# Attention output stored in runs, and the second expert's output sums done chunk by chunk: a three-stage kernel on one core

## The chip, the core and the metric

The kernel runs on one core of a Trainium2 chip. The time is the device time of one execution in microseconds; several runs are made and their median is given. A profile of one execution shows what each engine did: PE (TensorE, matmuls, with the weight loads apart as PEld), DVE (VectorE), ACT (ScalarE), POOL (GpSimd) and SP (SyncE, which issues the DMAs here). PSUM is the memory that TensorE writes its results to, in banks of 512 fp32 words in each of 128 partitions; SBUF is the working memory.

## The reference

Linear attention, then a dense layer, then a layer of eight experts of which each token uses one:

```python
# attention: batch 2, 8 heads, 576 tokens, head size 64, 128 features
q_p, k_p = phi(q * scale), phi(k * scale)
num = q_p @ (k_p.T @ v);  den = q_p @ sum(k_p) + 1e-6
x = (num / den) as [1152 tokens, 512]
# dense layer, d_ff 2048
h = x @ w_in;  x = (h * sigmoid(1.702 * h)) @ w_out
# experts: 8, d_ff 1024, capacity 288
logits = x @ w_gate;  e = argmax(logits);  gate = softmax(logits)[e]
y = relu(x @ w1[e]) @ w2[e]
out = gate * y, 0 for tokens beyond the capacity
```

## The kernel before

The 1152 tokens stand in columns: `x_hi` and `x_lo` hold x with the 512 features on partitions (four chunks c) and the tokens along the free axis. Each fp32 value is kept in two parts, hi and lo, and a product takes three matmuls (`mm3`, lines 98 to 100: hi by hi, hi by lo, lo by hi).

*Attention.* Each partition loads four consecutive tokens (JF = 4) of a head, so the results come with tokens 4n + j in block j. `do_X` (line 401) transposes four blocks into a PSUM bank and hands it to `x_out` (line 397): ACT casts the bank to `x_hi` (L398), DVE takes the difference as `x_lo` (L399). The last 64 tokens of each batch go through `do_Xm`. The PSUM banks for these steps, and for the transposes and products of the attention (`t`, `nps`, `xps`), come from `mbank`, two banks in turn; a bank is free again when x_lo has been made.

*Dense layer.* Tokens are worked on in four groups of 288 (GS). For a group G and a block m of 128 hidden features, `do_h` makes twelve matmuls into `h_ps` (two banks, tag A), ACT applies the activation, and `do_y` adds the products with `w_out` to four banks, one for each output chunk of 128 features. Groups 0, 1 and 3 run interleaved, group 2 after them. For groups 1 and 3 only the logits are made; `do_logits` copies the logits out of PSUM (`lgy`, L726, for groups 0 and 2) and transposes them (L733), and `pick_slot` chooses for groups 0 and 2 the expert that is worked on.

*Experts.* For the first expert (key 0, group 0) and the second (key 1, group 2) `do_h2` makes block m of the hidden layer (twelve matmuls, then ACT's relu at L863 and DVE's lo part at L864, which releases the `h_ps` bank), and `do_y2` adds block m to all four output chunks. Eight blocks (NF2 = 8) make an expert. In the main loop `do_y2` follows `do_h2` by two blocks. The second expert's weights come in eight pieces by DMA (`eraw`), each is split by ACT (`eh`, L850) and DVE (`el`, L851). At an expert's end `do_z_out` copies the four output banks to `z`, `z_rows` transposes 96 tokens of all four chunks into a bank, and `slot_rows` (line 922) puts the rows of the chosen tokens into `base`, scales them by the gate and issues the DMA to `out`. The tile scheduler decides the order on each engine from the order in which the code is written and from the data each instruction needs.

After that the code branches past the parts for further experts, which these inputs do not need.

Of the kernel before, what the change touches and what calls it, by code (L numbers as in the profile page):

```python
# [8 lines left out]
F32 = mybir.dt.float32  # L9
# [26 lines left out]
def linear_attention__moe__top1_moe_kernel(  # L36
# [156 lines left out]

    x_hi = xp.tile([128, KD, NT], F32R, name="x_hi")
    x_lo = xp.tile([128, KD, NT], F32R, name="x_lo")
    W = {}
    def w_pair(pool, kind, i):
        t = [pool.tile([128, 4, 512], F32R, tag=f"w{kind}{i}{s}", name=f"w{kind}{i}{s}") for s in "hl"]  # L200
# [196 lines left out]
    def x_out(hi, lo, ps):  # L397
        nc.scalar.copy(hi, ps)  # L398
        nc.vector.tensor_tensor(lo, ps, hi.bitcast(F32), ALU.subtract)  # L399

    def do_X(b, p, u):

        xr = xrs.pop((b, p, u))
        ps = mbank("xps")
        for j in range(JF):
            nc.tensor.transpose(ps[:, j * 128:(j + 1) * 128], xr[:, j], ident)
        hi, lo = (t[:, 2 * p + u, b * S:b * S + SF].rearrange("p (n j) -> p j n", j=JF)
                  for t in (x_hi, x_lo))
        x_out(hi, lo, ps.rearrange("p (j n) -> p j n", j=JF))

    def do_Xm(b, p):
        ps = mbank("xps")
        for u in range(2):
            nc.tensor.matmul(ps[:, u * 64:(u + 1) * 64], xms[p][:, u], fold, start=True, stop=True)
        hi, lo = (t[:, 2 * p:2 * p + 2, b * S + SF:(b + 1) * S] for t in (x_hi, x_lo))
        x_out(hi, lo, ps[:, :128].rearrange("p (u n) -> p u n", u=2))

    npre = len(P["dec"])
    wseq = [(kd, m) for m in range(NF) for kd in ("in", "out")]
# [178 lines left out]
    def slot(n, f):  # L598
        side.setdefault(round(n * 2) / 2, []).append(f)
# [9 lines left out]
        return [gp.tile([128, GS], F32R, tag=tag, name=tag, bufs=2) for tag in ("ghi", "glo")]  # L609

    def do_h(G, m, full=False):
        tk = slice(G * GS, G * GS + GS)
        hi, lo = w_in(m)
        ps = bank("A", "h_ps")
        for c in range(KD):
            mm3(ps[:, :GS], hi[:, c], lo[:, c], x_hi[:, c, tk], x_lo[:, c, tk],
                c == 0, c == KD - 1)
        if G % 2 and not full:
            g1 = gp.tile([128, GS], F32, tag="g1", name="g1", bufs=5)
            mark["a"] = nc.scalar.activation(g1, ps[:, :GS], ACTF.Gelu_apprx_sigmoid)  # L620
# [12 lines left out]
    def do_y(G, m):  # L633
        if m == 0:
            yps[G] = y_banks()
        ghi, glo = gs.pop((G, m))
        hi, lo = w_out(m)
        for c in range(KD):
            dc = slice(c * 128, c * 128 + 128)
            mm3(yps[G][c][:, :GS], hi[:, dc], lo[:, dc], ghi, glo, m == 0, m == NF - 1)  # L640
        if m == NF - 1:
            for c in range(KD):
                sl = (slice(None), c, slice(G * GS, G * GS + GS))
                y = yps[G][c][:, :GS]
                nc.scalar.copy(x_hi[sl], y)
                nc.vector.tensor_tensor(x_lo[sl], y, x_hi[sl].bitcast(F32), ALU.subtract)

    def do_lg(G, m):


        i = G - 1 + m % 2
        if i in lgq:
            run_lg()
        lgq[i] = (m, gs.pop((G, m)))
        if len(lgq) == 4 or (G, m) == (3, NF - 1):
            run_lg()
# [59 lines left out]
    def do_logits(G):  # L716
        if G % 2 == 0:
            ps = mbank("lg_ps")
            for c in range(KD):
                tk = slice(G * GS, G * GS + GS)  # L720
                nc.tensor.matmul(ps[:2 * E, :GS], wg[:, c].rearrange("p a e -> p (a e)"), x_hi[:, c, tk],
                                 start=(c == 0), stop=False)
                nc.tensor.matmul(ps[:E, :GS], wg[:, c, 0], x_lo[:, c, tk],
                                 start=False, stop=(c == KD - 1))
            t = gp.tile([2 * E, GS], F32, tag="g1", name="lgy", bufs=5)
            nc.scalar.copy(t, ps[:2 * E, :GS])  # L726
            n = 2 * E
# [124 lines left out]

    hs, zps = {}, {}

    def do_h2(key, m, wt, tok):
        ps = bank("A", "h_ps")
        hi, lo = wt[m // 4]
        fc = slice((m % 4) * 128, (m % 4) * 128 + 128)
        for c in range(KD):
            mm3(ps[:, :GS], hi[:, c, fc], lo[:, c, fc], x_hi[:, c, tok], x_lo[:, c, tok],  # L860
                c == 0, c == KD - 1)
        hhi, hlo = parts_tile(True)
        nc.scalar.activation(hhi, ps[:, :GS], ACTF.Relu)  # L863
        nc.vector.scalar_tensor_tensor(hlo, ps[:, :GS], 0.0, hhi.bitcast(F32), ALU.max, ALU.subtract)  # L864
        hs[key, m] = (hhi, hlo)
# [10 lines left out]
    def do_z_out(key, z):  # L876
        for c in range(KD):
            if c % 2:
                nc.scalar.copy(z[:, c], zps[key][c][:, :GS])
            else:  # L880
                nc.vector.tensor_copy(z[:, c], zps[key][c][:, :GS])

    def z_rows(z, j):
        ps = mbank("zt_ps")
        for c in range(KD):
            nc.tensor.transpose(ps[:TT, c * 128:(c + 1) * 128], z[:, c, j * TT:(j + 1) * TT], ident)
        return ps[:TT, :DM]
# [102 lines left out]
    slot(NSL + NF2 + 3, lambda: slot_rows(0, 0))  # L990
    slot(NSL + NF2 + 3, lambda: slot_rows(0, 1))
    slot(NSL + NF2 + 4, lambda: slot_rows(0, 2))

    def tokens(G):
        return slice(G * GS, (G + 1) * GS)

    for n in range(NSL + 2 * NF2 + 2):
        now[0] = n
        if n < NSL:
            do_h(*seq[n])  # L1000
        elif n < NSL + 2 * NF2:
            i, m = divmod(n - NSL, NF2)
            do_h2(i, m, st[f"w{i}"], tokens(2 * i))
        for f in side.pop(n - 0.5, []):
            f()
        if 2 <= n < NSL + 2:
            do_consume(*seq[n - 2])
# [6 lines left out]
    slot_z(1)
    slot_base(1)
    for j in range(TJ):
        slot_rows(1, j)
# [5 lines left out]
    with tc.If(n_left > 0):  # L1023
# [23 lines left out]
        with tc.For_i(0, n_left):  # L1047
# [64 lines left out]
```

## Time and profile before

| | us |
|---|---|
| median of 3 runs | 340.39 (340.26 to 340.43) |
| profiled execution, its own time | 339.27 |
| its span, first to last instruction | 337.5 |
| PE busy | 318.7 (94%) |
| DVE busy | 182.9 (54%) |
| ACT busy | 172.4 (51%) |
| POOL busy | 60.4 (18%) |

The span leaves out 1.8 us of the profiled execution's time. PE's busy time counts matmuls that overlap one another, and their ends are modelled, so what it did not do is read from its idle stretches. In a row of the waits, the instruction on the left waited for the one on the right of the arrow.

### The profile page before, as it was taken

What the parts mean: (1) busy time and instruction counts of PE and PEld (TensorE: products, weight loads), DVE (VectorE), ACT (ScalarE), POOL (GpSimd) and SP (SyncE); (2) the same over time, 40 slices, a digit from 0 to 9 for tenths busy, and PEclk for the clock granted to TensorE, in tenths of its full rate; (3) what the DMA queues carried; (4) which work ended last, traced back from release to release, by engine and by line L of the source; (5) the groups of instructions that cost most, each with busy time, mean ns of one, the idle gap of its engine ahead of it and who ended that gap; (6) DMA issues with size and microseconds to landing.
All of it is one profiled execution on the core that took longest, in us unless ns stands there. A gap on an engine that the chain in (4) does not pass through costs nothing.

```text
span 337.5 us, 6635 instructions
## 1 busy us (share of the span) xinstructions
PE 318.7 (94%) x2569; PEld 304.3 (90%) x2569; DVE 182.9 (54%) x438; ACT 172.4 (51%) x445; POOL 60.4 (18%) x83
## 2 busy tenths in 40 slices
PE   5999999989997999999999999999999999999991
PEld 4999998889896999999999999989999999998990
DVE  5678797887578775444446403117434123568322
ACT  2788888879834454444444434233634233165312
POOL 3110311122003444443443410000000001010000
PEclk9999999999999999999999999999999999999998
DMA  6999541401030545435441000523400000383202
GB/s 173 296 328 271 166 134 62 127 15 50 0 105 25 186 130 172 151 122 170 124 135 64 0 2 0 156 95 94 135 23 0 2 1 2 110 271 119 72 0 80
DMA packets 29079, 35.19 MB, mean 104 GB/s; under 512 B 5360, under 2 KB 23792, under 8 KB 29040
## 3 DMA queue, kind: packets, MB, share of 16 engines
q1 hardware_dynamic: 29040, 34.69, 33.0%
q8 instruction: 22, 0.36, 0.5%
q14 instruction: 17, 0.14, 0.1%
HBM read 32.33 MB, written 2.36 MB: 103 GB/s over the span
## 4 chain that ended last, share of the span: by engine, by line
PE 82%; ACT 6%; DVE 5%; DMA 4%; issue 1%; POOL 0%; SPq 0%; ACTq 0%; DVEq 0%
PE h_ps L98 12%; PE h_ps L99 12%; PE h_ps L100 12%; PE y L98 7%; PE y L100 7%; PE y L99 7%; PE kvp L339 4%; PE nps L364 3%; DMA eraw<-in_moe_w_dram 3%; PE tp L282 2%; PE pj L98 2%; ACT x_hi L398 2%; PE t L353 2%; PE pj L99 2%; PE pj L100 2%; PE wt_ps L492 2%
## 5 line engine op out<-in xcount | busy, mean ns | idle before, releaser
L627 DVE TENSOR_TENSOR glo<-g,ghi 128x288 fp32r<-128x288 f32 x27 | 12.9, 478 | 38.7 <-ACT g L626 38.7
L236 DVE TENSOR_SCALAR wf<-wraw 128x512 int32<-128x512 int32 x32 | 16.2, 512 | 26.9 <-POOL win2l L249 10.8
L620 ACT ACTIVATE g<-h_ps 128x288 f32<-128x288 f32 x32 | 13.2, 412 | 29.4 <-PE h_ps L100 24.5
L308 DVE TENSOR_REDUCE nb<-pj 128x4 f32<-128x512 f32 (+1 forms) x40 | 25.1, 631 | 3.9 <-PE pj L100 3.5
L851 DVE TENSOR_TENSOR el<-eraw,eh 128x1024 fp32r<-128x1024 f32 x16 | 19.5, 1222 | 12.0 <-ACT eh L850 12.0
L98 PE MATMUL pj<-om_hi,xh 128*128 128x256 f32 x72 | 24.6, 341 | 1.0 <-ACT qp L321 1.0
L242 DVE SCALAR_TENSOR_TENSOR wf<-wraw,wf 128x512 int32<-128x512 int32 x32 | 25.0, 784 | 0.5
L624 ACT ACTIVATE ghi<-h_ps 128x288 fp32r<-128x288 f32 x27 | 11.1, 412 | 24.5 <-PE h_ps L100 23.9
L850 ACT CAST eh<-eraw 128x1024 fp32r<-128x1024 f32 x16 | 16.7, 1049 | 13.4 <-PE h_ps L99 7.3
L321 ACT ACTIVATE qp<-pj,nb 128x128 f32<-128x128 f32 x72 | 21.8, 389 | 0.7 <-DVE nb L308 0.5
L239 DVE SCALAR_TENSOR_TENSOR wf<-wraw,wf 128x512 int32<-128x512 int32 x32 | 21.9, 691 | 0.2
L99 PE MATMUL pj<-om_lo,xh 128*128 128x256 f32 x72 | 21.7, 301 | 0.0
L321 ACT ACTIVATE kp<-pj,nb 128x128 f32<-128x128 f32 x72 | 21.6, 394 | 0.0
L100 PE MATMUL pj<-om_hi,xl 128*128 128x256 f32 x72 | 21.4, 298 | 0.0
L285 ACT CAST xh<-tp 128x256 fp32r<-128x256 f32 (+1 forms) x40 | 14.7, 369 | 11.7 <-PE tp L282 11.7
L98 PE MATMUL h_ps<-x_hi,win0h 128*128 128x288 f32 x64 | 20.1, 314 | 0.0
L100 PE MATMUL h_ps<-x_hi,win0l 128*128 128x288 f32 x64 | 19.2, 300 | 0.5 <-POOL win0l L249 0.5
L339 PE MATMUL kvp<-vt,kp 128*128 128x65 f32 (+1 forms) x144 | 19.7, 269 | 0.0
L98 PE MATMUL h_ps<-x_hi,win3h 128*128 128x288 f32 x64 | 19.6, 306 | 0.0
L98 PE MATMUL h_ps<-x_hi,win2h 128*128 128x288 f32 x64 | 19.6, 306 | 0.0
L98 PE MATMUL h_ps<-x_hi,win1h 128*128 128x288 f32 x64 | 19.4, 303 | 0.0
L98 PE MATMUL h_ps<-x_hi,eh 128*128 128x288 f32 x64 | 19.2, 300 | 0.0
(246 smaller groups left out, 1080.5 us busy)
## 6 DMA issues: line engine op xcount, KB each, us to landing
wraw<-in_moe_w_in_dram SPq DMA_DIRECT2D x16, 512.0 KB, 4.3
wraw<-in_moe_w_out_dram SPq DMA_DIRECT2D x16, 512.0 KB, 3.6
eraw<-in_moe_w_dram SPq DMA_DIRECT2D x16, 512.0 KB, 4.7
qk_raw<-in_v_dram SPq DMA_DIRECT2D x4, 512.0 KB, 5.2
qk_raw<-in_q_dram SPq DMA_DIRECT2D x4, 512.0 KB, 5.2
qk_raw<-in_k_dram SPq DMA_DIRECT2D x3, 512.0 KB, 5.1
out_dram<-zer SPq DMA_DIRECT2D x2, 576.0 KB, 6.3
out_dram<-base SPq DMA_DIRECT2D x6, 192.0 KB, 3.0
```

The source lines that it names most:

```text
L98: nc.tensor.matmul(o, lh, rh, start=start, stop=False)
L99: nc.tensor.matmul(o, lh, rl, start=False, stop=False)
L100: nc.tensor.matmul(o, ll, rh, start=False, stop=stop)
L236: nc.vector.tensor_scalar(f, high, 3, 0x3FFFFFF8, ALU.logical_shift_left, ALU.bitwise_and)
L239: nc.vector.scalar_tensor_tensor(f, high, -0x40000000, f, ALU.bitwise_and, ALU.bitwise_or)
L242: nc.vector.scalar_tensor_tensor(f, low, 29, f, ALU.logical_shift_right, ALU.bitwise_or)
L285: nc.scalar.copy(xh[:, :n], tp[:, :n])
L308: mark["M", s] = nc.vector.tensor_reduce(nb[:, :nj], pj[:, :nj * M].rearrange("p (a m) -> p a m", m=M), AX, ALU.min)
L321: nc.scalar.activation(t[:, i], pj[:, i * M:(i + 1) * M], ACTF.Exp, bias=nb[:, i:i + 1], scale=-1.0)
L339: nc.tensor.matmul(ps[:, o:o + n], kp[:, i], vts[p][:, u, c0:c0 + n], start=(f == 0), stop=(f == NU - 1))
L850: nc.scalar.copy(hi, tv)
L851: nc.vector.tensor_tensor(lo, tv, hi.bitcast(F32), ALU.subtract)
```

## The change

Two things are changed. First, x is kept with its tokens in runs: `x_hi` and `x_lo` get the shape [128, 4, JF, 288], and token 4i + j stands at (j, i). `do_X` writes runs of 128 words; a group of 288 tokens is then four runs of 72 words, which the matmuls on x read, and y of the dense layer is written back in the same way. All results of these matmuls have the order (j, i) in PSUM; where they leave PSUM (`z`, `lgy`, the copied logits) the copy reads them in the order (i, j) and writes rows in token order.

Second, the second expert's output sums are made in a new function `do_last`: chunk c is the outer loop and block m the inner one, so all eight hidden blocks are made before, and kept in two tiles of the weight buffer `win2` (`spare`). When a chunk is done, ACT copies it to `z`; in the middle of the next chunk's sums it is transposed, put into `base`, scaled and sent out. The first expert's rows are made inside the sums of chunk 0. The last chunk is copied in three parts by DVE and leaves in two DMAs.

```diff
-    x_hi = xp.tile([128, KD, NT], F32R, name="x_hi")
-    x_lo = xp.tile([128, KD, NT], F32R, name="x_lo")
+    x_hi = xp.tile([128, KD, JF, NI], F32R, name="x_hi")
+    x_lo = xp.tile([128, KD, JF, NI], F32R, name="x_lo")
...
-        hi, lo = (t[:, 2 * p + u, b * S:b * S + SF].rearrange("p (n j) -> p j n", j=JF)
-                  for t in (x_hi, x_lo))
+        hi, lo = (t[:, 2 * p + u, :, b * BI:b * BI + 128] for t in (x_hi, x_lo))
         x_out(hi, lo, ps.rearrange("p (j n) -> p j n", j=JF))
...
-        hi, lo = (t[:, 2 * p:2 * p + 2, b * S + SF:(b + 1) * S] for t in (x_hi, x_lo))
-        x_out(hi, lo, ps[:, :128].rearrange("p (u n) -> p u n", u=2))
+        hi, lo = (t[:, 2 * p:2 * p + 2, :, b * BI + 128:(b + 1) * BI].rearrange("p u j i -> p u i j")
+                  for t in (x_hi, x_lo))
+        x_out(hi, lo, ps[:, :128].rearrange("p (u i j) -> p u i j", u=2, j=JF))
...
-            mm3(ps[:, :GS], hi[:, c], lo[:, c], x_hi[:, c, tk], x_lo[:, c, tk],
+            mm3(ps[:, :GS], hi[:, c], lo[:, c], x_hi[:, c, :, tk], x_lo[:, c, :, tk],
...
-            nc.scalar.copy(t, ps[:2 * E, :GS])
+            nc.scalar.copy(rows_of(t), in_order(ps[:2 * E, :GS]))
...
+        if key == 1 and m:
+            for s in "hl":
+                if s not in spare:
+                    spare[s] = pool_of["in", 2].tile([128, NF2 - 1, GS], F32R, tag=f"win2{s}", name=f"hh{s}")
+            hhi, hlo = spare["h"][:, m - 1], spare["l"][:, m - 1]
+        else:
+            hhi, hlo = parts_tile(True)
...
+    def do_last(wt):
+        z, base = scratch(1)
+        nc.gpsimd.memset(base, 0.0)
+        zps[1] = y_banks()
...
+        def chunk(c):
+            dc = slice(c * 128, c * 128 + 128)
+            ps = mbank("zt_ps")
+            for j in range(TJ):
+                nc.tensor.transpose(ps[:TT, j * 128:(j + 1) * 128], z[:, c, j * TT:(j + 1) * TT], ident)
+            nc.vector.copy_predicated(base[:, :, dc], mk.unsqueeze(2).to_broadcast([TT, TJ, 128]),
+                                      ps[:TT, :TJ * 128].rearrange("p (j d) -> p j d", j=TJ))
+            nc.vector.tensor_tensor(base[:, :, dc], base[:, :, dc],
+                                    gw[:, g0:g0 + TJ].unsqueeze(2).to_broadcast([TT, TJ, 128]), ALU.mult)
+            nc.sync.dma_start(out=rows[:, :, dc], in_=base[:, :, dc])
+        half = NF2 // 2
+        for c in range(KD):
+            sums(c, range(half))
+            if c:
+                chunk(c - 1)
+            else:
+                slot_rows(0, 0)
+                slot_rows(0, 1)
+            sums(c, range(half, NF2))
+            if c == 0:
+                slot_rows(0, 2)
+            if c < KD - 1:
+                nc.scalar.copy(rows_of(z[:, c]), in_order(zps[1][c][:, :GS]))
...
+        for j in range(TJ):
+            nc.vector.tensor_copy(rows_of(zl[j]), in_order(zps[1][c][:, :GS])[:, j * TT // JF:(j + 1) * TT // JF])
+        for j, ps in enumerate(pss):
+            nc.tensor.transpose(ps[:TT, 0:128], zl[j], ident)
+            nc.vector.copy_predicated(base[:, j, dc], mk[:, j:j + 1].to_broadcast([TT, 128]), ps[:TT, 0:128])
+            if j < TJ - 1:
+                nc.scalar.activation(base[:, j, dc], base[:, j, dc], ACTF.Copy, scale=gw[:, g0 + j:g0 + j + 1])
+            else:
+                nc.vector.tensor_scalar(base[:, j, dc], base[:, j, dc], gw[:, g0 + j:g0 + j + 1], None, ALU.mult)
+        nc.sync.dma_start(out=rows[:, 0, dc], in_=base[:, 0, dc])
+        nc.sync.dma_start(out=rows[:, 1:, dc], in_=base[:, 1:, dc])
```

In the attention the order on every engine stays as it is. In the second expert it changes. On TensorE before, behind the block m = 2 of the second expert (`h_ps`, with `eh` and `el` the expert's weights) its first y block begins, one output bank (`y_4100` to `y_4103`) after the other; the waits are those on an engine's counter:

```order
L99 MATMUL h_ps<-x_lo,eh 128x288
L100 MATMUL h_ps<-x_hi,el 128x288
L98 MATMUL y_4100<-ghi,eh 128x288 [waits DVE_49,Activation_49]
L99 MATMUL y_4100<-glo,eh 128x288
L100 MATMUL y_4100<-ghi,el 128x288
L98 MATMUL y_4101<-ghi,eh 128x288 [waits Activation_49]
```

In the changed kernel the block m = 3 follows m = 2 at once, and behind it stand one y matmul (`y_4177` is the bank of chunk 0) and the block m = 4:

```order
L102 MATMUL h_ps<-x_lo,eh 128x288
L103 MATMUL h_ps<-x_hi,el 128x288
L101 MATMUL y_4177<-ghi,eh 128x288 [waits DVE_49,Activation_49]
L101 MATMUL h_ps<-x_hi,eh 128x288 [waits DVE_49]
L102 MATMUL h_ps<-x_lo,eh 128x288
```

So the y matmuls that stood between the blocks of the second expert now stand behind all of them, and each of the blocks m = 4 to 7 begins with a wait for DVE.

On DVE before, from the split of the second expert's fifth weight piece (`el`) to the kernel's last copies; `z` are the copies of the first and later of the second expert's output banks:

```order
L851 TENSOR_TENSOR el<-eraw,eh 128x1024
L864 SCALAR_TENSOR_TENSOR ghl<-h_ps,ghl 128x288
L881 COPY z<-y_3732 128x288
L851 TENSOR_TENSOR el<-eraw,eh 128x1024
L881 COPY z<-y_3734 128x288
L851 TENSOR_TENSOR el<-eraw,eh 128x1024
L864 SCALAR_TENSOR_TENSOR glo<-h_ps,ghi 128x288
L851 TENSOR_TENSOR el<-eraw,eh 128x1024
L864 SCALAR_TENSOR_TENSOR glo<-h_ps,ghi 128x288
L927 COPY_PREDICATED base<-p_mk,zt_ps 96x512 x2
```

In the changed kernel, from the seventh piece's split on; `hhl` are the lo parts of the second expert's blocks m = 2 and later:

```order
L863 TENSOR_TENSOR el<-eraw,eh 128x1024
L884 SCALAR_TENSOR_TENSOR hhl<-h_ps,hhh 128x288
L863 TENSOR_TENSOR el<-eraw,eh 128x1024
L884 SCALAR_TENSOR_TENSOR hhl<-h_ps,hhh 128x288 x5
L1004 COPY_PREDICATED base<-p_mk,zt_ps 96x512 x3
L931 COPY_PREDICATED base<-p_mk,zt_ps 96x3x128
L933 TENSOR_TENSOR base<-base,gw 96x3x128
```

The order of the splits and the lo parts among themselves is the same as before; what follows them is new. On TensorE the second expert's twelve transposes stood behind its last y matmul; now three stand inside the sums of each of the chunks 1 to 3, and three at the end.

## Rows read from the trace of the kernel before

**Rows 1.** Stretches: us, busy PE, PEld, DVE, ACT, POOL, then clock, DMA share, GB/s.

```profile
30.00:111.00 81.00, 74.75 (x625) 70.69 (x625) 64.14 (x165) 61.99 (x179) 13.58 (x18) 1.00 0.28 87
111.00:304.00 193.00, 192.97 (x1563) 184.68 (x1562) 85.75 (x205) 79.59 (x180) 40.56 (x40) 1.00 0.29 92
304.00:309.00 5.00, 4.26 (x31) 3.83 (x30) 4.64 (x8) 3.75 (x6) 0.00 (x0) 1.00 0.51 193
328.40:337.50 9.10, 1.71 (x13) 0.96 (x11) 2.20 (x4) 2.46 (x4) 0.00 (x0) 0.87 0.25 74
```

**Rows 2.** Waits of TensorE from 28 to 112 us: total, times, longest.

```profile
PE nps L368 <- DVE x_lo L399: 1.5, 2, 0.8
PE xps L414 <- DVE xm L394: 1.1, 1, 1.1
PE pj L98 <- ACT qp L321: 1.0, 2, 0.8
PE t L353 <- DVE den L382: 0.8, 2, 0.4
PE tp L282 <- DVE xl L292: 0.6, 1, 0.6
PE h_ps L100 <- POOL win0l L249: 0.5, 1, 0.5
PE wg_ps L502 <- DVE xm L394: 0.3, 1, 0.3
PE t L353 <- DVE x_lo L399: 0.2, 1, 0.2
```

**Rows 3.** Groups by line and form: busy us, mean ns, idle before.

```profile
L98 PE MATMUL h_ps<-x_hi,eh 128*128 128x288 f32 x64 | 19.2, 300 | 0.0
...
L355 ACT COPY qt<-t 128x512 f32<-128x512 f32 x16 | 9.5, 594 | 4.1 <-PE t L353 3.8
...
L399 DVE TENSOR_TENSOR x_lo<-xps,x_hi 128x512 fp32r<-128x512 f32 x8 | 8.8, 1095 | 7.1 <-ACT x_hi L398 7.0
L398 ACT CAST x_hi<-xps 128x512 fp32r<-128x512 f32 x8 | 8.7, 1089 | 2.9 <-PE xps L406 2.8
...
L384 DVE TENSOR_TENSOR xr<-nps,den 128x256 f32<-128x256 f32 x16 | 6.7, 418 | 0.1
...
L399 DVE TENSOR_TENSOR x_lo<-xps,x_hi 128x128 fp32r<-128x128 f32 x4 | 1.1, 278 | 0.0
...
L726 ACT COPY lgy<-lg_ps 16x288 f32<-16x288 f32 x2 | 0.8, 390 | 2.9 <-PE lg_ps L723 2.9
```

**Rows 4.** Timeline near 102 to 107 us: start, duration, engine, instruction.

```profile
101.98 1.09 ACT L398 CAST x_hi<-xps 128x512 fp32r<-128x512 f32 x1
...
103.58 1.28 POOL L249 TENSOR_TENSOR win0l<-wf,win0h 128x512 fp32r<-128x512 f32 x1 [24.36 <-ACT win0h L248]
...
104.90 1.50 DVE L236 TENSOR_SCALAR wf<-wraw 128x512 int32<-128x512 int32 x1 [0.24 <-POOL win0l L249]
```

**Rows 5.** Timeline of the second expert's begin, 306 to 312 us.

```profile
306.25 1.05 ACT L850 CAST eh<-eraw 128x1024 fp32r<-128x1024 f32 x1 [0.86 <-DMA eraw<-in_moe_w_dram]
...
307.33 1.22 DVE L851 TENSOR_TENSOR el<-eraw,eh 128x1024 fp32r<-128x1024 f32 x1 [0.36 <-ACT eh L850]
...
308.48 0.45 DVE L864 SCALAR_TENSOR_TENSOR glo<-h_ps,ghi 128x288 fp32r<-128x288 f32 x1
...
311.90 0.38 PE L98 MATMUL h_ps<-x_hi,eh 128*128 128x288 f32 x1
```

**Rows 6.** The chain that ended last, from 304 us: start, us, what.

```profile
315.31 0.43 PE zt_ps L886 x4
...
328.31 0.13 PE y L100
...
331.56 0.72 ACT base L928
```

**Rows 7.** The output DMAs of both experts: count, KB each, us to landing.

```profile
out_dram<-base SPq DMA_DIRECT2D x6, 192.0 KB, 3.0
```

More of the change, by code (lines that the diff above doesn't have):

```diff
@@ L66, in linear_attention__moe__top1_moe_kernel @@
     SF = JF * 128
+    NI = NT // JF
+    GI = GS // JF
+    BI = S // JF
     NU = 18
@@ L191, in linear_attention__moe__top1_moe_kernel, with tokens, in_order, rows_of @@
     om_lo2 = om_lo.rearrange("p a m -> p (a m)")
-    x_hi = xp.tile([128, KD, NT], F32R, name="x_hi")
-    x_lo = xp.tile([128, KD, NT], F32R, name="x_lo")
+    def tokens(G):
+        return slice(G * GI, (G + 1) * GI)
+    def in_order(t):
+        return t.rearrange("p (j i) -> p i j", j=JF)
+    def rows_of(t):
+        return t.rearrange("p (i j) -> p i j", j=JF)
+    x_hi = xp.tile([128, KD, JF, NI], F32R, name="x_hi")
+    x_lo = xp.tile([128, KD, JF, NI], F32R, name="x_lo")
     W = {}
@@ L611, in do_h @@
     def do_h(G, m, full=False):
-        tk = slice(G * GS, G * GS + GS)
+        tk = tokens(G)
         hi, lo = w_in(m)
@@ L642, in do_y @@
             for c in range(KD):
-                sl = (slice(None), c, slice(G * GS, G * GS + GS))
-                y = yps[G][c][:, :GS]
+                sl = (slice(None), c, slice(None), tokens(G))
+                y = yps[G][c][:, :GS].rearrange("p (j i) -> p j i", j=JF)
                 nc.scalar.copy(x_hi[sl], y)
@@ L658, in do_lg @@
             held_t.append(gp.tile([128, GS], F32, tag="g1", name="lgt", bufs=5))
-            nc.scalar.copy(held_t[0], held.pop()[:, :GS])
+            nc.scalar.copy(rows_of(held_t[0]), in_order(held.pop()[:, :GS]))
     lgq, held_t, now = {}, [], [0]
@@ L719, in do_logits @@
             for c in range(KD):
-                tk = slice(G * GS, G * GS + GS)
-                nc.tensor.matmul(ps[:2 * E, :GS], wg[:, c].rearrange("p a e -> p (a e)"), x_hi[:, c, tk],
+                tk = tokens(G)
+                nc.tensor.matmul(ps[:2 * E, :GS], wg[:, c].rearrange("p a e -> p (a e)"), x_hi[:, c, :, tk],
                                  start=(c == 0), stop=False)
-                nc.tensor.matmul(ps[:E, :GS], wg[:, c, 0], x_lo[:, c, tk],
+                nc.tensor.matmul(ps[:E, :GS], wg[:, c, 0], x_lo[:, c, :, tk],
                                  start=False, stop=(c == KD - 1))
             t = gp.tile([2 * E, GS], F32, tag="g1", name="lgy", bufs=5)
-            nc.scalar.copy(t, ps[:2 * E, :GS])
+            nc.scalar.copy(rows_of(t), in_order(ps[:2 * E, :GS]))
             n = 2 * E
@@ L853, in linear_attention__moe__top1_moe_kernel @@
     hs, zps = {}, {}
+    spare = {}
     def do_h2(key, m, wt, tok):
@@ L859, in do_h2 @@
         for c in range(KD):
-            mm3(ps[:, :GS], hi[:, c, fc], lo[:, c, fc], x_hi[:, c, tok], x_lo[:, c, tok],
+            mm3(ps[:, :GS], hi[:, c, fc], lo[:, c, fc], x_hi[:, c, :, tok], x_lo[:, c, :, tok],
                 c == 0, c == KD - 1)
-        hhi, hlo = parts_tile(True)
+        if key == 1 and m:
[5 more added lines that the diff above has]
+            hhi, hlo = parts_tile(True)
         nc.scalar.activation(hhi, ps[:, :GS], ACTF.Relu)
@@ L878, in do_z_out @@
             if c % 2:
-                nc.scalar.copy(z[:, c], zps[key][c][:, :GS])
+                nc.scalar.copy(rows_of(z[:, c]), in_order(zps[key][c][:, :GS]))
             else:
-                nc.vector.tensor_copy(z[:, c], zps[key][c][:, :GS])
+                nc.vector.tensor_copy(rows_of(z[:, c]), in_order(zps[key][c][:, :GS]))
     def z_rows(z, j):
@@ L887, in z_rows, with sums @@
         return ps[:TT, :DM]
+    def do_last(wt):
+        z, base = scratch(1)
+        nc.gpsimd.memset(base, 0.0)
+        zps[1] = y_banks()
+        mk = st["mk", 1].bitcast(I32)
+        r0 = 2 * GS
+        g0 = 2 * TJ
+        rows = out[r0:r0 + GS, :].rearrange("(j p) d -> p j d", p=TT)
+        def sums(c, ms):
+            dc = slice(c * 128, c * 128 + 128)
+            for m in ms:
+                hhi, hlo = hs[1, m]
+                hi, lo = wt[2 + m // 4]
+                mm3(zps[1][c][:, :GS], hi[:, m % 4, dc], lo[:, m % 4, dc], hhi, hlo, m == 0, m == NF2 - 1)
+        def chunk(c):
+            dc = slice(c * 128, c * 128 + 128)
+            ps = mbank("zt_ps")
[19 more added lines that the diff above has]
+                nc.scalar.copy(rows_of(z[:, c]), in_order(zps[1][c][:, :GS]))
+        c = KD - 1
+        dc = slice(c * 128, c * 128 + 128)
+        pss = [mbank("zt_ps"), mbank("zt_ps"), bank("A", "zt_ps")]
+        zl = [z[:, c, 0:TT]] + [pool_of["out", 0].tile([128, 2048], F32, tag=f"wout0{s}", name="zl")[:, 0:TT] for s in "hl"]
+        for j in range(TJ):
[9 more added lines that the diff above has]
+        nc.sync.dma_start(out=rows[:, 1:, dc], in_=base[:, 1:, dc])
@@ L989, in linear_attention__moe__top1_moe_kernel @@
     slot(NSL + NF2 + 1, lambda: slot_base(0))
[L990 to L995, printed above, removed]
     for n in range(NSL + 2 * NF2 + 2):
@@ L1009, in linear_attention__moe__top1_moe_kernel @@
             i, m = divmod(n - 2 - NSL, NF2)
-            do_y2(i, m, st[f"w{i}"])
+            if i == 0:
+                do_y2(i, m, st[f"w{i}"])
+            elif m == NF2 - 1:
+                do_last(st[f"w{i}"])
         for f in side.pop(n, []):
             f()
[L1014 to L1017, printed above, removed]
     n_left = nc.values_load(st["all"][0:1, 0:1], min_val=0, max_val=NP)
@@ L1069, in linear_attention__moe__top1_moe_kernel @@
                 if m < NF2:
-                    do_h2("x", m, wt, ds(gv * GS, GS))
+                    do_h2("x", m, wt, ds(gv * GI, GI))
                 if m:
```

## The prediction

> **What bounds the kernel now.** I read the busy times by stretch first [rows 1]. From 111 to 304 us TensorE works 192.97 of 193.00 us: there only less TensorE work helps. It stands still in three places. From 30 to 111 us, the attention with the first layer's start mixed in, it works 74.75 of 81.00 us, so 6.25 us are idle. From 304 to 309 us, where the second expert begins, 0.74 of 5.00 us are idle. From 328.4 us on it has almost nothing left to do, and 9.1 us pass. The granted clock is 1.00 in all of these until the end, so no idle time here costs clock too.
>
> The waits of TensorE in the first stretch [rows 2] say who ends them: x_lo (L399) twice, 1.5 us, and once 0.2; den (L382) twice, 0.8 us; qp (L321) 1.0; xl (L292) 0.6; win0l 0.5; xm 1.1 and 0.3. The two waits put down to den I count to x_lo: den is a small operation right behind x_lo on DVE, and what TensorE needs at both places is the PSUM bank that x_lo reads last.
>
> Then the price of x_out by form [rows 3]: the 128x512 cast to x_hi takes 1089 ns on ACT, while the plain 128x512 copy out of PSUM (L355) takes 594. The DVE half takes 1095 ns for 512 elements; 128 elements take 278 and 256 take 418, that is 1.09 ns each more, which makes some 700 for 512. Both slow ones write every fourth word.
>
> **The change, part by part.**
>
> *Storing in runs.* The eight large x_out pairs write runs of 128 words instead. I price them like the contiguous rows: ACT 1.09 to 0.59, DVE 1.09 to 0.70, together 0.9 us sooner to the release of the bank, eight times [rows 3]. It lies on the path only where TensorE waits for it. The waits on x_lo (1.5, 0.2, and den's 0.8) are five, the longest 0.8, all below 0.9: they go, -2.5 us. Near 67 us qp's wait of 0.8 stands behind x_hi in ACT's order and loses 0.5; the xl wait of 0.6 stands behind x_lo on DVE, which comes 0.9 sooner while TensorE arrives 0.5 sooner, -0.4. At 107 us the xm wait is the end of a chain: two x_hi casts, win0h, win0l on POOL at 103.58, wf on DVE at 104.90 with 1.50 us, xm [rows 4]. Two casts shorter by 0.5 move it by 1.0, of which 0.8 is counted already in the wait on x_lo before it: -0.2. Sum -3.6 us. Bounds: only the waits that name x_lo, -1.7; all idle time of the stretch, -6.2. From 111 us on TensorE is the bound, so what is won stays won.
>
> Here a rule of the Trainium skill can be laid beside the rows. "SBUF — State Buffer", section "Door 1: The DMA port swizzle", says that SBUF works in lines of 16 bytes and that accesses which go to a new line each time pay. A stride of four fp32 words is just that case, and the rows agree with 1089 against 594 ns; by the rule the runs would be as cheap as I took them.
>
> The four small x_out pairs (128x128) now write with a large stride. At the strided rows' surcharge, 0.50 us for 512, that is 0.13 us each on ACT and DVE. No wait of TensorE names one of them and other work covers them: 0, bound +0.5.
>
> *Reading x.* All matmuls on x read four runs of 72 columns instead of one of 288. No row shows a moving operand in runs. I take 0, since inside a run nothing changes; the other bound is a rival below. The writes of y to x (L645, L646) go in runs of 72 words, taken at 0 for the same reason.
>
> *Logits.* lgy now reads PSUM with four words 288 bytes apart. No row shows that. Bounds: 0.39 us as now, or the ratio of the strided write, 1089/594, which makes 0.71. Between them +0.15 each. The transposes right behind it wait for it twice on TensorE's path (groups 0 and 2): +0.3 us, bounds 0 and +0.65. lgt (groups 1 and 3) is copied long before it is needed: 0.
>
> *The second expert.* TensorE's order above shows five blocks of twelve matmuls on x in a row with one y matmul between. What paced them before was the y work in between; now the fifth block (m = 4) needs the bank of m = 2, and that is released by the DVE instruction behind the split of the expert's seventh weight piece. Its times don't depend on TensorE: the eh cast starts at 306.25 when the DMA lands, el at 307.33, the hlo part at 308.48 with 0.45, end 308.93 [rows 5]. With 0.1 us to get to TensorE, m = 4 starts at 309.03. Before, it started at 311.90 [rows 5], but by then 23 more y matmuls and 8 transposes were done. These cost 23 x 0.13 = 3.0 and 8 x 0.11 = 0.9 us (four transposes 0.43, one matmul 0.13 [rows 6]). Nine transposes of the second expert, 1.0 us, stand ahead of its last matmul now, and stood behind it before. So the last y matmul ends at 328.44 - 2.87 + 3.0 + 0.9 + 1.0 = 330.5, against 328.44 [rows 6]: +2.1 us. Put as idle time: about 1.8 us of wait for DVE in place of the 0.74. Of the later blocks none waits: there are two banks, a block takes 12 x 0.13 = 1.6 us, and one ACT and one DVE operation of under 0.5 us each release one.
>
> The hidden blocks are written to win2, which the first expert's fourth y block reads last, well before; the zeroing of base on POOL has nothing behind it: 0 for both.
>
> Queued behind this wait on TensorE are the rest of the expert and the first expert's transposes, which come at about 309.0 + 4 x 1.6 + 1.4 = 316.8, still over 10 us from the end, so their outputs stay covered.
>
> *The tail.* Before: from 328.44 to the end of the last scaling, 331.56 + 0.72 = 332.28, are 3.84 us [rows 6], then to the span's end 5.2. After: three DVE copies of 96 columns (0.24 each by the 1.09 ns above, 0.34 if the strided PSUM read costs), 0.6 to 0.9 in a row; three predicated copies of 128 columns, 0.28 and two steps of 0.2; the scaling of 128 columns, taken like the DVE row, 0.28 [rows 3]. The first predicated copy may start before the third z copy ends, or just behind it. That is 1.6 to 1.9 us; with starts of 0.04 between them I take 1.8: -2.0. The three chunks before are out by then, since each has a chunk of 24 matmuls, 3.1 us, to cover a cast, three transposes and two DVE operations of some 0.6 us each. On SP only the output DMAs are left then, so those moved pass nothing. Of the second expert's DMAs the last carry 48 and 96 KB instead of 192, which take 3.0 us to land [rows 7]; since the end also waits for the engines' last branches, 0, bound -0.9.
>
> So the reordering of the sums earns 2.0 us in the tail and pays 2.1 before it: +0.1, bounds -1.5 and +1.0.
>
> Sum: -3.6 + 0.3 + 0.1 = -3.2 us. The profiled execution took 339.27 us and would take 336.1. It lies 1.1 us below the median of the runs, 340.39, so I forecast 337.2.
>
> **The rivals.**
>
> 1. *Runs cost the moving operand.* The trace has 15 groups like L98's with eh, 64 each [rows 3]: 960 matmuls on x, nearly all in the stretch where TensorE never rests. At 3.3 ns each, 3.2 us over 960, the gain is gone; at a tenth of the 0.13 us spacing, 13 ns, they cost 12.5 us and the kernel takes 349.7 us. For it: nothing hides there. Against it: in runs of 72 the engines that I can price pay per word of a bad stride, not per run. Chance 0.08.
>
> 2. *The attention gives back.* ACT and DVE work 62 and 64 of the 81 us, and each wait removed may leave a smaller one on another row. If only the waits naming x_lo go, -1.7: 340.39 - 1.7 + 0.4 = 339.1. Chance 0.17.
>
> 3. *Strided reads of PSUM are dear.* The lgy copies cost +0.65 and the tail's copies +0.3 more than a contiguous read would: 0.5 over the sum, 337.7, and the z copies of chunks 0 to 2 remain hidden. Chance 0.15. A sentence of the skill speaks for this: "PSUM — Partial Sum Buffer", section "Specifications (TRN2)", says that any access there that is not contiguous slows matmuls significantly; no run here shows whether it holds for ACT and DVE.
>
> 4. *The new wait does not come, or more idle time goes.* If the weights' last pieces are split sooner, m = 4 starts up to 1.8 us sooner, or the attention's idle time goes nearly whole: 335.2. Chance 0.12.
>
> The forecast, with 336.2 to 338.3, has 0.48. From 335.2 to 339.4 hold all but rival 1 and the outer part of 2 and 4. A measurement of this kernel tells some 0.2%, 0.7 us, from no change. Faster by more: forecast, 3, 4 and most of 2, 0.81. Same: rest of 2, 0.09. Slower: rival 1, with a little for a wait that I did not see, 0.10.
>
> **What would show it.** x_hi at about 0.6 and x_lo at 0.7 us mean; idle time of TensorE from 30 to some 107 us near 2.6 instead of 6.25 us, no wait of nps or t on x_lo. Matmuls on x spaced 0.13 us as before, else rival 1. lgy between 0.39 and 0.71. In the second expert a wait of TensorE of nearly 2 us for the DVE part of m = 2, and from the last y matmul to the last scaling 1.8 us. The forecast is wrong if the idle time of the attention stays above 4.5 us, or if the stretch from 111 to 304 grows by more than 1 us.

## The result, and the profile after

| | before | changed | ratio (95% interval) |
|---|---|---|---|
| median (lowest to highest), us | 340.32 (4 runs, 339.16 to 340.43) | 335.75 (4 runs, 334.22 to 336.88) | 0.987 (0.983 to 0.991) |
| profiled execution: time, span | 339.27, 337.5 | 336.30, 334.5 | |

The forecast was 337.2 us with a range of 335.2 to 339.4: the sign is right and the time lies in the range, but the medians lie 4.6 us apart where 3.2 were worked out, and the kernel came there by another sum. Two later sets of runs gave ratios of 0.983 (0.975 to 0.990) and 0.985 (0.983 to 0.988).

First the groups of x_out by line and form in the changed kernel (busy us, mean ns, idle before), which answer to [rows 3]:

```profile
L411 DVE TENSOR_TENSOR x_lo<-xps,x_hi 128x512 fp32r<-128x512 f32 x8 | 5.5, 692 | 3.6 <-ACT x_hi L410 3.3
L410 ACT CAST x_hi<-xps 128x512 fp32r<-128x512 f32 x8 | 4.7, 590 | 2.9 <-PE xps L418 2.8
...
L410 ACT CAST x_hi<-xps 128x128 fp32r<-128x128 f32 x4 | 1.6, 395 | 4.6 <-PE xps L425 4.5
L411 DVE TENSOR_TENSOR x_lo<-xps,x_hi 128x128 fp32r<-128x128 f32 x4 | 1.5, 383 | 0.7 <-ACT x_hi L410 0.7
L949 ACT COPY z<-y 128x288 f32<-128x288 f32 x3 | 1.2, 392 | 5.1 <-PE y L103 5.1
```

590 and 692 ns are the 0.59 and 0.70 us of the forecast; the small pairs grew by 0.13 and 0.105 us. The last row, a copy that reads PSUM with four words 288 bytes apart, costs 392 ns, no more than a plain one.

The waits of TensorE from 28 to 112 us (total, times, longest), against [rows 2]:

```profile
PE xps L425 <- DVE xm L406: 1.1, 1, 1.1
PE pj L101 <- ACT qp L333: 0.6, 2, 0.4
PE h_ps L103 <- POOL win0l L261: 0.6, 1, 0.6
```

All waits on x_lo and den are gone, and so is the one on xl. The stretches (columns as in [rows 1]):

```profile
30.00:108.00 78.00, 75.65 (x642) 72.80 (x642) 62.31 (x167) 59.56 (x180) 14.40 (x19) 1.00 0.30 93
108.00:300.00 192.00, 191.99 (x1554) 183.74 (x1553) 84.92 (x205) 79.15 (x179) 39.69 (x39) 1.00 0.29 95
300.00:310.00 10.00, 8.12 (x49) 7.89 (x49) 5.55 (x8) 4.56 (x9) 0.00 (x0) 0.83 0.08 30
326.00:334.50 8.50, 1.58 (x11) 1.05 (x9) 2.14 (x8) 0.69 (x2) 0.00 (x0) 0.85 0.18 44
```

The attention has 2.35 us of idle time left (2.6 were forecast). The long middle is full at clock 1.00: reading x in four runs of 72 costs nothing, and the matmuls on x there start 0.133 us apart as before. The third row holds a surprise: 1.88 idle us, as forecast, but also a mean granted clock of 0.83 (1.00 is 2.4 GHz, 0.50 is 1.2 GHz). Microsecond by microsecond:

```profile
302.00:303.00 1.00, 0.00 (x0) 0.00 (x0) 1.00 (x2) 1.00 (x3) 0.00 (x0) 1.00 0.00 0
303.00:304.00 1.00, 0.14 (x1) 0.14 (x2) 1.00 (x3) 0.74 (x2) 0.00 (x0) 1.00 0.00 0
304.00:305.00 1.00, 1.00 (x7) 1.00 (x8) 1.00 (x2) 0.00 (x0) 0.00 (x0) 0.78 0.00 0
305.00:306.00 1.00, 1.00 (x6) 1.00 (x5) 0.30 (x1) 0.00 (x0) 0.00 (x0) 0.50 0.00 0
306.00:307.00 1.00, 1.00 (x6) 1.00 (x5) 0.00 (x0) 0.41 (x1) 0.00 (x0) 0.50 0.00 0
307.00:308.00 1.00, 1.00 (x6) 1.00 (x5) 0.46 (x1) 0.00 (x0) 0.00 (x0) 0.51 0.00 0
308.00:309.00 1.00, 1.00 (x9) 1.00 (x9) 0.00 (x0) 0.12 (x1) 0.00 (x0) 1.00 0.00 0
```

After the wait TensorE works for some 0.7 us at 2.4 GHz and then for more than three at 1.2 GHz; fourteen matmuls start 0.24 us apart instead of 0.13, which is 1.5 us lost. DVE's timeline (start, duration) shows what the wait is for:

```profile
302.21 1.23 DVE L863 TENSOR_TENSOR el<-eraw,eh 128x1024 fp32r<-128x1024 f32 x1
303.35 0.45 DVE L884 SCALAR_TENSOR_TENSOR hhl<-h_ps,hhh 128x288 fp32r<-128x288 f32 x1
```

and TensorE's timeline shows the block m = 4, which waits for it:

```profile
303.86 0.40 PE L101 MATMUL h_ps<-x_hi,eh 128*128 128x288 f32 x1 [1.88 <-DVE hhl L884]
```

This is the wait that the forecast put at 1.8 us, at the same place and behind the same split ([rows 5] for its parts before). The tail, from the last y matmul on, in the timeline:

```profile
326.64 0.29 PE L103 MATMUL y<-hhh,el 128*128 128x288 f32 x1
326.97 0.26 DVE L955 COPY z<-y 128x96 f32<-128x96 f32 x1 [0.41 <-PE y L103]
327.14 0.41 DVE L955 COPY zl<-y 128x96 f32<-128x96 f32 x2
...
327.63 0.72 DVE L958 COPY_PREDICATED base<-p_mk,zt_ps 96x128 f32<-96x128 int32 x3
328.02 0.69 ACT L960 ACTIVATE base<-base,gw 96x128 f32<-96x128 f32 x2 [4.16 <-DVE base L958]
328.39 0.28 DVE L962 TENSOR_SCALAR base<-base,gw 96x128 f32<-96x128 f32 x1
```

From 326.97, when the first copy begins, to 328.71, when the last scaling (ACT's) ends, are 1.7 us; before it took 3.84 from that point [rows 6].

For the experiments I divide each span at three points that all kernels have: the first x_hi cast (33.64 us before, 33.63 after), the last one, behind the wait on xm (107.83 and 102.60), and the first thing that the chain of work does behind the last y matmul (328.44 and 326.97). The casts, first before, then after:

```profile
33.64 1.08 ACT L398 CAST x_hi<-xps 128x512 fp32r<-128x512 f32 x1
107.83 0.27 ACT L398 CAST x_hi<-xps 128x128 fp32r<-128x128 f32 x1 [3.82 <-PE xps L414]
...
33.63 0.59 ACT L410 CAST x_hi<-xps 128x512 fp32r<-128x512 f32 x1
102.60 0.40 ACT L410 CAST x_hi<-xps 128x128 fp32r<-128x128 f32 x1 [3.80 <-PE xps L425]
```

The first part is then the attention, 74.19 and 68.97 us; the second everything from there to the last sum, 220.61 and 224.37; the third the tail. What lies ahead of the first cast differs by up to 1.3 us between the profiles (33.19 to 34.46 us) and by 0.6 between the three of the changed kernel, so it is left out.

### The profile page after: what moved, and what is told of

Same layout as the page of the kernel before. It is cut to its first block, busy times and chain, and to the rows that moved or that the text cites. A ratio compares the mean times of both kernels' runs of the same rounds, so it can differ in the third digit from the quotient of the medians.

```text
span 334.5 us, 6647 instructions
## 1 busy us (share of the span) xinstructions
PE 318.1 (95%) x2569; PEld 305.1 (91%) x2569; DVE 180.6 (54%) x446; ACT 168.3 (50%) x445; POOL 60.3 (18%) x83
## 4 chain that ended last, share of the span: by engine, by line
PE 85%; DMA 4%; DVE 3%; ACT 3%; issue 1%; SPq 1%; POOL 0%; ACTq 0%
PE h_ps L101 13%; PE h_ps L102 12%; PE h_ps L103 12%; PE y L102 7%; PE y L103 7%; PE y L101 7%; PE kvp L351 4%; PE nps L376 4%; DMA eraw<-in_moe_w_dram 3%; PE pj L101 2%; PE t L365 2%; PE pj L102 2%; PE pj L103 2%; PE tp L294 2%; PE wt_ps L504 2%; PE lgt_ps L684 1%
## 5 line engine op out<-in xcount | busy, mean ns | idle before, releaser
L248 DVE TENSOR_SCALAR wf<-wraw 128x512 int32<-128x512 int32 x32 | 14.5, 459 | 28.7 <-POOL win2l L261 10.8
L101 PE MATMUL h_ps<-x_hi,eh 128*128 128x288 f32 x64 | 19.9, 310 | 1.9 <-DVE hhl L884 1.9
L102 PE MATMUL pj<-om_lo,xh 128*128 128x256 f32 x72 | 21.1, 293 | 0.0
L102 PE MATMUL h_ps<-x_lo,eh 128*128 128x288 f32 x64 | 19.7, 307 | 0.0
L103 PE MATMUL h_ps<-x_hi,el 128*128 128x288 f32 x64 | 19.6, 307 | 0.0
```

Source lines behind the costliest of these rows:

```text
L248: nc.vector.tensor_scalar(f, high, 3, 0x3FFFFFF8, ALU.logical_shift_left, ALU.bitwise_and)
```

## The experiments

**The runs alone.** x in runs, the second expert's sums as before:

```diff
...
-            if i == 0:
-                do_y2(i, m, st[f"w{i}"])
-            elif m == NF2 - 1:
-                do_last(st[f"w{i}"])
+            do_y2(i, m, st[f"w{i}"])
...
```

> x is stored in runs and read in runs as in the changed kernel; the second expert's sums stay as before. Theory: the runs earn 5.2 us in the attention (the first cast behind it came at 101.94 in place of 107.17 us) and nothing is lost elsewhere, so the time is 340.3 - 5.2 = 335.1 us, with two short waits of TensorE at the second expert's begin (0.74 us in sum before) and a granted clock of 1.00 there. Rival 1, the forecast's own size: the attention earns 3.6 us, 336.7. Rival 2: a part of the 5.2 is given back where the second expert waits for its weights, since they come no sooner; then the idle time there is more than 0.74 us, and the time 336 or more.

Measured: 335.03 us, ratio 0.986 (0.983 to 0.990) to 339.77. The attention takes 68.98 us, as in the changed kernel, and the part behind it 220.76 against 220.61. So the 5.2 us are real and all but 0.15 us of them are kept there; both rivals fall.

**The sums alone.** The old order of x, with `do_last`: the changed kernel with the layout undone.

> x stays in its old order, only the second expert's sums are made chunk by chunk. Theory: the reordering alone loses. TensorE waits 1.9 us ahead of the block m = 4, the granted clock falls to 0.50 for some 3.4 us behind this wait, and the tail from the last y matmul to the last scaling takes 1.8 in place of 3.84 us. In the changed kernel these three came to +2.2 us beside the attention's -5.2, so 340.3 + 2.2 = 342.5 us. Rival 1, the forecast: the reordering comes to +0.1, 340.4 us, with a clock of 1.00 in the second expert. Rival 2: the fall of the clock belongs to x in runs and not to the wait; then the wait is there, the clock stays at 1.00, and the time is 340.9.

Measured: 340.28 us, ratio 1.0018 (1.0002 to 1.0034), that is +0.5 us (+0.1 to +1.2). The attention takes 74.18 us. The part behind it takes 222.67, that is 2.06 us more than before (the forecast said 2.1), the tail to the last scaling's end is 2.1 us shorter. The wait is there, the fall of the clock isn't; TensorE's timeline at the wait, and the stretches behind it:

```profile
309.37 0.40 PE L101 MATMUL h_ps<-x_hi,eh 128*128 128x288 f32 x1 [2.04 <-DVE hhl L884]
```

```profile
310.00:311.00 1.00, 1.00 (x10) 1.00 (x9) 0.81 (x2) 0.00 (x0) 0.00 (x0) 1.00 0.00 0
311.00:312.00 1.00, 1.00 (x10) 1.00 (x9) 0.29 (x1) 0.41 (x1) 0.00 (x0) 1.00 0.00 0
312.00:313.00 1.00, 1.00 (x10) 1.00 (x9) 0.17 (x1) 0.15 (x1) 0.00 (x0) 1.00 0.00 0
```

My theory, which took the fall for a fixed part of the change, is wrong by 2 us. The two rivals, +0.1 and +0.6 us, both lie in the measured interval. The parts of rival 1, the forecast's own sum, agree with the measured ones (+2.1 and -2.1); but the wait with a clock of 1.00 is just what rival 2 said, so whether the fall needs x in runs isn't settled by this kernel.

**The wait removed.** The splits of the last three weight pieces are put behind the blocks' relu and lo part:

```diff
-        slot(NSL + 5 + i // 2, lambda i=i: split_e(st["w1"], i, 1))
+        if i < 5:
+            slot(NSL + 5 + i // 2, lambda i=i: split_e(st["w1"], i, 1))
+        else:
+            slot(NSL + (10 if i == 5 else 11), lambda i=i: late_split(i))
...
+    def late_split(i):
+        with tc.issue_after(mark["hh"].ins):
+            with tc.issue_after(mark["hl"].ins):
+                split_e(st["w1"], i, 1)
```

`mark["hh"]` and `mark["hl"]` are the latest block's relu and lo part.

> The changed kernel with the splits of the second expert's sixth, seventh and eighth weight pieces put behind the relu and lo part of the blocks m = 2 (sixth) and m = 3 (the others). Theory: the block m = 4 then finds its bank free; the longest wait of TensorE in the second expert is under 0.5 us, the granted clock stays at 1.00, and both the 1.88 us of wait and the some 1.5 us of slow clock are saved: 335.8 - 3.0 = 332.8 us. Rival 1: the clock falls there whatever the wait is, for instance with the end of a long stretch without rest: only the wait is saved, 334.2. Rival 2: the wait moves to a later block, since the pieces have to be split some time: 335.8.

Measured: 333.03 us, ratio 0.980 (0.977 to 0.983). The lo part of m = 2 now stands ahead of the split, in DVE's timeline:

```profile
300.57 0.46 DVE L889 SCALAR_TENSOR_TENSOR hhl<-h_ps,hhh 128x288 fp32r<-128x288 f32 x1 [0.90 <-ACT hhh L888]
301.51 1.23 DVE L863 TENSOR_TENSOR el<-eraw,eh 128x1024 fp32r<-128x1024 f32 x1 [0.48 <-ACT eh L862]
```

and of the waits of TensorE from 290 us on one is left, in the tail:

```profile
PE zt_ps L962 <- DVE z L960: 0.4, 1, 0.4
```

The part behind the attention takes 220.90 us: the 2.06 us are back but for 0.3, without giving up the shorter tail. The wait was thus nearly the whole price of the reordering. It lay ahead of the block m = 4, as forecast; it was not needed, and with the splits put off it did not move to a later block. The theory (332.8) holds in time and in kind, but no fall of the clock is shown to have been saved.

**The wait filled.** Fourteen matmuls whose result nobody reads, ahead of m = 4:

```diff
+            if (i, m) == (1, 3):
+                fl = mbank("fl_ps")
+                for r in range(14):
+                    nc.tensor.matmul(fl[:, :GS], st["w1"][0][0][:, r % 4, 384:512],
+                                     x_hi[:, r % 4, :, tokens(2)], start=True, stop=True)
```

> The changed kernel with 14 more matmuls on x (0.13 us apart, 1.87 us) written to a bank that nobody reads, ahead of the block m = 4. They fill the wait and take nothing off it: m = 4 starts when it did. Theory: the clock fell because TensorE stood still; now it stays at 1.00 and the some 1.5 us of slow clock are saved, 334.3 us. Rival 1: the clock falls there anyway, as after a long stretch of full load; the time stays at 335.8. Rival 2: the matmuls themselves come late or hold something up, and the time is over 336.

Measured: 335.82 us, ratio 0.987 (0.984 to 0.990); no wait and a clock of 1.00 in its profile, and 222.88 us behind the attention. That is what the sums alone took with the wait and without the fall (222.67). For the clock this decides nothing: the fall was absent there too. The time is that of rival 1, but its reason is not: the clock did not fall in this profile.

**One half at a time.** Either x_lo or x_hi goes back to token order, written and read with a stride of four words. For x_lo:

```diff
-    x_lo = xp.tile([128, KD, JF, NI], F32R, name="x_lo")
+    x_lo = xp.tile([128, KD, NT], F32R, name="x_lo")
+    def by_run(t, c, tok):
+        a = tok.start * JF
+        return t[:, c, a:a + GS].rearrange("p (i j) -> p j i", j=JF)
...
-            mm3(ps[:, :GS], hi[:, c], lo[:, c], x_hi[:, c, :, tk], x_lo[:, c, :, tk],
+            mm3(ps[:, :GS], hi[:, c], lo[:, c], x_hi[:, c, :, tk], by_run(x_lo, c, tk),
```

> The changed kernel, but x_lo stays in token order: DVE writes it with a stride of four words, and TensorE reads it so (four runs of 72 words, each with a stride of 16 bytes); x_hi stays in runs. The order on every engine is that of the changed kernel; the loop for further experts, which is not entered, takes a fixed group. Theory: DVE's half of x_out costs 1.09 in place of 0.69 us again and ACT's stays at 0.59, so of the 0.9 us that each pair won 0.5 are left, and of the attention's 5.2 us some 2.9; the first cast behind the wait on xm comes at about 104.9 us, and the time is 335.8 + 2.3 = 338.1. Rival 1: ACT's half alone is what the waits saw; then nothing is lost, 335.8. Rival 2: the strided moving operand costs TensorE time: 320 matmuls read x_lo, and each 13 ns (a tenth of their spacing) is 4.2 us more, 342 or above, seen as a spacing over 0.133 us on L102.

> The mirror image: x_hi stays in token order, written by ACT and read by TensorE with a stride of four words, x_lo is in runs. DVE's half reads x_hi with the stride too. The order on every engine is that of the changed kernel; the loop for further experts, which is not entered, takes a fixed group. Theory: ACT's half costs 1.09 again, DVE's 0.69, so 0.4 of 0.9 us are left, and of the attention's 5.2 us some 2.3: 335.8 + 2.9 = 338.7. Rival 1: DVE's half pays the stride too, since it reads x_hi with it (1.09 us in place of 0.69): all 5.2 are lost, 341.0. Rival 2: the strided moving operand costs TensorE time; here 640 matmuls read x_hi, so a cost is twice that of the other kernel.

Measured: 373.58 us, ratio 1.095 (1.089 to 1.102), and 418.48 us, ratio 1.227 (1.220 to 1.235). Rival 2 of both holds, and far beyond the tenth that I had put down. TensorE's timeline with x_lo strided (L102 reads x_lo):

```profile
150.42 0.29 PE L101 MATMUL h_ps<-x_hi,win0h 128*128 128x288 f32 x1
150.56 0.42 PE L102 MATMUL h_ps<-x_lo,win0h 128*128 128x288 f32 x1
150.80 0.31 PE L103 MATMUL h_ps<-x_hi,win0l 128*128 128x288 f32 x1
150.95 0.29 PE L101 MATMUL h_ps<-x_hi,win0h 128*128 128x288 f32 x1
```

From L102 to the next start are 0.24 us in place of 0.133, with the granted clock at 1.00. Three matmuls take 0.53 us, not 0.40; 320 times 0.13 is 42 us, near the 39 by which the time grew. (The changed kernel of the same set, below, took 334.46 us.) With x_hi strided, two of three pay, and it grew by 84. This is rival 1 of the prediction with the wrong pattern: what costs is the stride between words, not the number of runs. The Trainium skill's "SBUF — State Buffer", section "Door 1: The DMA port swizzle", says that accesses which go to a new 16-byte line each time pay. The trace agrees for TensorE's moving operand too, with 0.24 against 0.133 us; the prediction had applied it to ACT and DVE alone.

The attention ahead of the first matmuls on x can still be compared. From the first x_hi cast to the eighth (82.94 us in the changed kernel) are 52.91 us before, 49.31 in the changed kernel, 49.71 with x_lo strided, 52.89 with x_hi strided. So with 0.5 of the 0.9 us per pair, 3.2 of 3.6 us are kept. The theory, by which the attention keeps 2.9 of 5.2 us, would have kept 2.0 of these 3.6: it is wrong here too, and rival 1, by which ACT's half is what the waits saw, is nearer. With x_hi strided all is lost, as its rival 1 said, for DVE reads x_hi with the stride and pays again:

```profile
L416 DVE TENSOR_TENSOR x_lo<-xps,x_hi 128x512 fp32r<-128x512 f32 x8 | 8.6, 1080 | 7.1 <-ACT x_hi L415 7.0
```

**The changed kernel again, and beside the late splits.** Two more profiles of the changed kernel, the second in one set with the kernel with the late splits.

> The changed kernel as it is, profiled once more. Theory: the wait ahead of m = 4 comes every time (1.9 us), since what ends it hangs on the weights' splits; the fall of the granted clock behind it comes in some executions only, as the kernel with the sums alone waited 2.0 us with the clock at 1.00. Without the fall the span from the cast behind the wait on xm to the end is 230.4 us in place of 231.9. Rival: in this kernel the fall belongs to the wait, comes again, and the time is 336 or more whenever it is profiled.

> The changed kernel as it is, beside the kernel with the late splits. Theory: a wait of 1.3 to 1.9 us ahead of m = 4, according to when the weights land, and a median of some 335 us; whether the clock falls behind the wait is open (once in two profiles so far). Rival: the wait is gone in some executions, and the median is that of the late splits, 333.

> The kernel with the late splits once more, beside the changed kernel on one chip. Theory: no wait of TensorE at m = 4, so it saves the wait (1.3 to 1.9 us so far) and, in the executions in which the clock falls behind the wait, some 1.5 us more: 1.3 to 2.5 us under the changed kernel's median, and a smaller spread. From the cast behind the wait on xm to the span's end 228.4 us, as in its first profile. Rival: its lead was that of a chip or of a few runs; then the two medians lie within 0.7 us.

Measured: the changed kernel 334.46 (334.02 to 337.06) and 335.29 us (334.77 to 336.67), the late splits 333.22 us (332.77 to 334.34), ratio to before 0.979 (0.977 to 0.982). On one chip the late splits lead by 2.1 us, with no overlap of the two sets of times, and this version beats the kernel before and the changed one. The wait of the changed kernel took 1.3 us in the one profile and 1.8 in the other, here the other's, and the stretches behind it:

```profile
304.36 0.40 PE L101 MATMUL h_ps<-x_hi,eh 128*128 128x288 f32 x1 [1.80 <-DVE hhl L884]
```

```profile
304.00:306.00 2.00, 1.64 (x12) 1.64 (x13) 1.81 (x3) 0.37 (x2) 0.00 (x0) 1.00 0.00 0
306.00:308.00 2.00, 2.00 (x17) 2.00 (x16) 0.46 (x1) 0.55 (x2) 0.00 (x0) 1.00 0.00 0
308.00:310.00 2.00, 2.00 (x17) 2.00 (x16) 0.55 (x2) 0.69 (x2) 0.00 (x0) 1.00 0.00 0
```

No fall in either. The parts behind the attention are 222.18 and 222.79 us.

## Why the prediction was right, and where it was wrong

*Storing in runs: right in kind, too small.* The prices were right to 0.01 us, and it was the bank's earlier release that counted. Forecast -3.6 us, measured -5.2, the same in the runs alone. The step that was mis-sized is "The waits on x_lo ... are five ...: they go, -2.5 us", with its neighbours. I summed the idle time that the profile shows, but the time lost at a wait is longer. TensorE's timeline before the change, at the first of them:

```profile
35.13 0.36 PE L98 MATMUL pj<-om_hi,xh 128*128 128x256 f32 x1
35.92 0.33 PE L353 MATMUL t<-ident,qp 128*128 128x128 f32 x1 [0.42 <-DVE den L382]
```

The matmul ahead starts at 35.13 and is drawn 0.36 us long, so 0.42 us are left to 35.92. In the changed kernel the same two start at 35.12 and 35.32, 0.20 us apart: 0.59 us were lost, not 0.42, since a matmul's drawn duration is longer than the time after which the next can start. Place by place (instruction that waited, start in both kernels):

| waited for it | before | after | idle shown | sooner by |
|---|---|---|---|---|
| t | 35.92 | 35.32 | 0.42 | 0.65 |
| t | 43.92 | 42.90 | 0.21 | 0.43 |
| t | 58.02 | 56.67 | none | 0.33 |
| pj, for qp | 67.18 | 65.40 | 0.82, 0.45 left | 0.44 |
| tp, for xl | 69.86 | 67.27 | 0.58 | 0.74 |
| wg_ps | 70.45 | 67.48 | 0.26 | 0.38 |
| t | 81.80 | 78.25 | 0.42 | 0.65 |
| nps | 88.91 | 84.40 | 0.74 | 0.89 |
| nps | 102.73 | 97.45 | 0.80 | 0.90 |

The last column adds what the next matmuls win as well (0.05 to 0.07 us); it sums to 5.4, of which 0.2 are lost again in small steps behind the two nps. The five waits that I priced at 2.5 us gave 3.5, one that no view names gave 0.33, and the place near 67 us gave 1.56 in place of 0.9. The wait on xm at the end stayed at 1.05 us; the 0.2 us put there did not come. The small pairs cost what was said, and no wait names them.

*Reading x in runs: right.* 0, with 0.133 us between matmuls and a full middle stretch. Rival 1 is refuted for runs of 72.

*Logits: wrong by 0.3 us.* lgy takes 388 ns against 390 [rows 3], and ACT's strided copies to z 392 ns, as many as the contiguous ones of the sums alone: reading PSUM 288 bytes apart costs ACT nothing. DVE's copies to z take 448 ns, against 451 there. Rival 3 falls. The Trainium skill's "PSUM — Partial Sum Buffer", section "Specifications (TRN2)", says that non-contiguous access to PSUM slows matmuls. No run here tests that: the matmuls still write their banks contiguously.

*The second expert: right, with something not foreseen.* The wait came at the named instruction, 1.9 us long in place of 1.8, and +2.06 us where 2.1 were worked out (the sums alone). In the changed kernel the part behind the attention grew by 1.6 and 2.2 us where the clock held and by 3.8 where it fell. The sentence "no idle time here costs clock too" is the step that failed in the profiled execution: it held for the waits before, and in this execution the clock fell behind the longer one, which cost some 1.5 us. That the wait is the cause of the fall is not shown.

*The tail: right.* -2.1 us against -2.0. The end behind it did not gain: from the last scaling to the span's end are 5.8 us in place of 5.2. The runs alone, whose tail is the old one, also show 5.9, so this is not the work of the smaller pieces. That they win nothing agrees with the issues of the last stretch (KB, us to landing): the 96 KB take no less than the median of the 192 KB [rows 7]. No run shows that the last branches hold the end, as the forecast had it.

```profile
out_dram<-base SPq DMA_DIRECT2D x1, 96.0 KB, 3.5
out_dram<-base SPq DMA_DIRECT2D x1, 48.0 KB, 1.5
```

Sum by the runs: -5.2 in the attention, 0 for logits, +2.1 and -2.1 in the second expert and the tail, +0.6 in the end: -4.6, which is also the difference of the medians. (The 0.6 rests on the one profile of before; what its end takes in other executions is not known.) In the profiled execution the second expert cost +3.8, with the fall of the clock, and the whole came to -3.0, near the -3.2 forecast. That nearness is luck: a fall that the forecast didn't have hid what the attention won beyond it. The range was partly luck as well: one of the later medians, 334.46, lies under its lower end. The forecast's likeliest case missed by the attention's 1.6 us; of the rivals, the second half of 4, that the attention's idle time goes nearly whole, came nearest. The change's two halves are worth -4.7 and +0.5 us by themselves; the second pays only once its wait is taken out, and then 2.0 us.

Still open is when the clock falls. Of four profiles with a wait of 1.3 to 2.0 us ahead of m = 4, one shows the fall. The changed kernel's 14 executions lie in two heaps, nine from 334.0 to 335.6 us and five from 336.3 to 337.1, and the profiled one with the fall is in the second. Over the whole execution the mean clock was 0.990 or 0.991 in those five and 0.993 to 0.997 in the nine, so the other four may have fallen too. It isn't shown: kernels without this wait have such executions as well (the runs alone 336.32 us at 0.990, the late splits 334.34 at 0.987), and the mean also holds the fall in the tail, where it costs TensorE nothing.

## What to carry to other kernels

At TensorE a wait cost more than the idle time drawn, because matmuls are drawn longer than they hold their engine: measure it from start to start against the same pair of instructions where nothing waits. In SBUF, let every engine meet runs of consecutive words; if one side has to be strided, let it be the read of a copy out of PSUM, which paid nothing here, and not the matmul's moving operand, which paid 0.11 us each time. When loops are exchanged, look for work of another stage that the old order placed in between and that now stands ahead of the only instruction that frees a buffer; here, moving three splits turned a loss of 0.5 us (339.77 us before, 340.28 with the sums alone) into a gain of 2.0 (335.03 us with the runs alone, 333.03 with late splits).

## What the runs showed of the hardware

- A moving operand of 288 fp32 words in four runs of 72 consecutive words: matmuls 0.133 us apart, as from one run. The same 288 words with a stride of four: 0.24 us (granted clock 1.00 in both).
- DVE pays for a strided operand in SBUF whether it writes it (1.10 us) or reads it (1.08 us); with both in runs it is 0.69. ACT and DVE read PSUM at 288-byte steps without a price (128x288: 392 and 448 ns, against 392 and 451 contiguous).
- The clock of TensorE dropped once from 2.4 to 1.2 GHz behind a wait of 1.88 us, not at once but some 0.7 us into the work that followed, for more than 3 us. Waits of 1.26, 1.80 and 2.04 us at the same place were followed by a clock of 1.00, so the wait's length alone doesn't tell whether it falls.
